# A windowed-attention and highway-FFN kernel: PSUM by a fixed plan of eight banks, and a searched order of issue

## The chip, the cores and the metric

One NeuronCore of one Trainium2 chip. The metric is the device time of one execution in microseconds (us); lower is better. The granted clock is the share of full speed that the profile gives for PE, 1.00 at full speed. The engines are PE (matmul; PEld is its weight loads), DVE (vector), ACT (scalar), POOL (GpSimd, which also issues the loads here) and SP (which issues the stores).

## The reference

```python
def _attn_ref(q, k, v):                      # q, k, v: 8 batches, 8 heads, 576 rows, 64 columns
    scores = scale * np.matmul(q, k.transpose(0, 1, 3, 2))
    ...                                      # + slope[h] * -|i - j|; only 0 <= i - j < 128 is kept
    attn = np.exp(scores - max) / sum
    return np.matmul(attn, v)

def _moe_ref(x, w_h, w_t, b_t):              # x: 4608 x 512, the attention output
    H = np.maximum(x @ w_h, 0.0)
    T = 1.0 / (1.0 + np.exp(-(x @ w_t + b_t)))
    return T * H + (1.0 - T) * x
```

## The kernel before

It works on four pairs of batches (m = 0 to 3). For each pair, Q, K and V come in by casting loads from POOL's queue; PE transposes Q and K; scores go through exp on ACT and a mask on DVE; PV gives x (after a normalising step on DVE); then each 128-row tile of x goes through the FFN: transpose (`xp`), two products (`h` with the first weight, `z` with the second, plus a bias matmul), tanh, and the elementwise rest. Each such step is a piece ("node"); a small planner inside the kernel simulates the engines and writes down one order of all pieces, and that order is what each engine executes, strictly in sequence.

PSUM is a rotating pool of four tiles of two banks each. Everything takes such a tile, also what fills one bank:

```python
psp = ctx.enter_context(tc.tile_pool(name="ps", bufs=BUFS["ps"], space=PSUM))     # BUFS["ps"] is 4

def ps_tile(dt=F32):
    return psp.tile([P, 2, 512 if dt == F32 else 1024], dt, name="ps")
...
def f_h(m, kind, gi, i):                     # a whole two-bank tile for one 128 x 512 product
    if i == 0:
        AH[m, kind, gi] = ps_tile()
    for c in range(NCK):
        nc.tensor.matmul(out=AH[m, kind, gi][:, i, :], lhsT=XT[m, kind, gi][:, i, c, :],
                         rhs=wH[:, c, :], start=c == 0, stop=c == NCK - 1)
```

The V loads, and what clears V's buffers (a column of ones, and zeros under the last, half-filled chunk):

```python
def load_v(m, c):
    n = min(P, S - c * P)
    nc.gpsimd.dma_start(
        out=VA[m % 2][0:n, c, :, :, 0:D].rearrange("s r h d -> s (r h) d"),
        in_=v[2 * m : 2 * m + 2, :, c * P : c * P + n, :].rearrange("r h s d -> s (r h) d"),
    )
def c_ones(i):
    nc.vector.memset(VA[i][:, :, :, :, D : D + 1], 1.0)
def c_vpad(i):
    nc.vector.memset(VA[i][D:P, 4, :, :, :], 0.0)
```

The softmax here doesn't subtract the row's maximum and nothing guards it: scores larger than these inputs give would overflow.

## Time and profile before

| | before |
|---|---|
| time, median of the first 3 runs | 185.03 us (184.45 to 185.9) |
| profiled span | 183.9 us |
| PE busy / idle | 155.0 / 28.9 us |
| PE idle before 41 us | 15.0 us |
| last PE matmul ends | 177.0 us |
| changes of PE's tile shape (counted in its stream) | 151 |

How to read it: the share of busy time alone says "PE, 84%". What decides is where the idle 28.9 us lie and what ended each gap; PE executes in a fixed order, so one late operand holds everything behind it. The prediction shows the lines.

### The profile page before, as it was taken

The page shows a single profiled execution, that of the slowest core. Times are in us where ns is not written, and L with a number is a line of the kernel's source. Part 1 is how long each engine was busy: PE and PEld are TensorE (multiplying, and loading weights), DVE is VectorE, ACT ScalarE, POOL GpSimd, SP SyncE. Part 2 cuts the span into 40 slices and gives each one's busy share as a digit, 9 for nine tenths or more (in the row PEclk, how much of TensorE's full clock was granted, in tenths as well). Part 3 has the DMA queues.
Part 4 walks back from the last instruction along what each step waited for, and adds up shares of the span by engine and source line. Part 5 has one row for each costly group of instructions (what it writes and reads, how often), then busy time and mean ns, then how long its engine had stood idle before and what let it go on. Part 6 is the DMA issues. An engine that isn't in the chain of part 4 may idle for free.

```text
span 183.9 us, 5244 instructions
## 1 busy us (share of the span) xinstructions
PE 155.0 (84%) x2132; PEld 93.9 (51%) x2132; DVE 141.6 (77%) x253; ACT 127.8 (69%) x178; POOL 121.5 (66%) x132
## 2 busy tenths in 40 slices
PE   0286886779999957997999999999998999999950
PEld 0264655655564524675554565665444666555510
DVE  5339885699999893697688999799899788866770
ACT  2558595753889953879779889786998888445510
POOL 7994123979999945984269953544487787667540
PEclk9999999999999996999999999999999999999995
DMA  4999999999999999999997994142212322243543
GB/s 157 225 187 198 200 199 176 138 132 92 127 207 228 210 200 205 135 187 225 208 135 96 178 159 90 45 103 61 57 45 74 93 66 74 74 103 99 137 128 94
DMA packets 70167, 25.50 MB, mean 139 GB/s; under 512 B 48128, under 2 KB 65024, under 8 KB 70144
## 3 DMA queue, kind: packets, MB, share of 16 engines
q0 software_dynamic: 62832, 14.68, 113.6%
q1 hardware_dynamic: 7312, 10.49, 21.3%
q8 instruction: 16, 0.26, 0.6%
q14 instruction: 7, 0.06, 0.1%
HBM read 30.41 MB, written 9.44 MB: 217 GB/s over the span
## 4 chain that ended last, share of the span: by engine, by line
PE 38%; DMA 26%; DVE 16%; POOL 7%; ACT 5%; issue 3%; SPq 1%; POOLq 0%; DVEq 0%; ACTq 0%
DMA kl<-in_k_dram 24%; PE ps L460 10%; PE ps L443 9%; DVE pt L363 6%; PE ps L386 6%; PE ps L270 5%; PE ps L328 5%; DVE x L403 4%; POOL ot L484 3%; DMA out_dram<-ot 3%; ACT pt L344 2%; PE ps L462 2%; DVE uu L450 2%; POOL ql L110 2%; PE ps L426 2%
## 5 line engine op out<-in xcount | busy, mean ns | idle before, releaser
L344 ACT ACTIVATE pt<-ps,bias 128x1024 bf16<-128x1024 f32 (+1 forms) x80 | 73.4, 951 | 9.1 <-PE ps L328 8.4
L484 POOL TENSOR_TENSOR ot<-uu,x 128x512 f32<-128x512 bf16 x35 | 49.7, 1421 | 30.4 <-DVE uu L478 28.9
L363 DVE TENSOR_TENSOR pt<-pt,mk 128x2048 bf16<-128x2048 bf16 (+1 forms) x40 | 47.8, 1210 | 0.7 <-ACT pt L344 0.5
L460 PE MATMUL ps<-wT,xt 128*128 128x512 bf16 x144 | 38.0, 387 | 1.2 <-DVE uu L450 0.7
L443 PE MATMUL ps<-wH,xt 128*128 128x512 bf16 x144 | 37.2, 380 | 0.6 <-DVE uu L450 0.3
L122 POOL DMA_DIRECT2D va<-in_v_dram x20 | 22.2, 1117 | 14.3 <-DMA kl<-in_k_dram 8.2
L450 DVE SCALAR_TENSOR_TENSOR uu<-ps,x 128x512 bf16<-128x512 f32 x36 | 24.8, 688 | 7.7 <-PE ps L443 7.3
L468 ACT ACTIVATE tt<-ps 128x512 f16<-128x512 f32 x36 | 21.5, 598 | 11.6 <-PE ps L462 11.1
L328 PE MATMUL ps<-qt,kt 64*128 64x256 bf16 (+2 forms) x384 | 27.2, 254 | 1.8 <-DVE kt L295 1.4
L473 POOL TENSOR_SCALAR tt<-tt 128x512 f16<-128x512 f16 x32 | 23.1, 722 | 5.6 <-ACT tt L468 5.5
L435 ACT COPY xt<-ps 128x512 bf16<-128x512 bf16 x36 | 21.0, 586 | 8.1 <-PE ps L426 7.2
L403 DVE TENSOR_TENSOR x<-ps,rd 128x256 bf16<-128x256 f32 (+3 forms) x40 | 25.5, 637 | 1.4
L386 PEld LDWEIGHTS <-pt 128*128 128x128 bf16 (+1 forms) x576 | 21.2, 101 | 8.0 <-issue 1.8
L386 PE MATMUL ps<-va,pt 128*128 128x65 bf16 (+1 forms) x576 | 24.1, 196 | 1.3 <-ACT kt L295 0.4
L295 ACT COPY kt<-ps 128x1024 bf16<-128x1024 bf16 x13 | 13.1, 1012 | 14.4 <-PE ps L270 8.4
L289 DVE COPY qt<-ps 128x1024 bf16<-128x1024 bf16 x16 | 10.9, 687 | 14.2 <-PE ps L270 10.9
L478 DVE TENSOR_TENSOR uu<-uu,tt 128x512 bf16<-128x512 bf16 x36 | 16.6, 462 | 4.9 <-POOL tt L473 2.9
L270 PE MATMUL ps<-ident,ql 128*64 128x128 bf16 (+1 forms) x320 | 13.3, 242 | 8.3 <-DMA ql<-in_q_dram 7.5
L443 PEld LDWEIGHTS <-xt 128*128 128x128 bf16 x144 | 12.1, 97 | 14.4 <-issue 2.8
L460 PEld LDWEIGHTS <-xt 128*128 128x128 bf16 x144 | 12.4, 99 | 13.7 <-issue 3.9
L328 PEld LDWEIGHTS <-kt 64*128 64x128 bf16 x384 | 12.8, 97 | 12.6 <-issue 7.0
L270 PE MATMUL ps<-ident,kl 128*64 128x128 bf16 (+1 forms) x320 | 12.8, 242 | 6.6 <-DMA kl<-in_k_dram 5.6
(46 smaller groups left out, 127.9 us busy)
## 6 DMA issues: line engine op xcount, KB each, us to landing
out_dram<-ot SPq DMA_DIRECT2D x128, 64.0 KB, 1.8
va<-in_v_dram POOLq DMA_DIRECT2D x16, 256.0 KB, 10.8
ql<-in_q_dram POOLq DMA_DIRECT2D x3, 1024.0 KB, 14.6
kl<-in_k_dram POOLq DMA_DIRECT2D x3, 1024.0 KB, 18.8
ql<-in_moe_w_h_dram SPq DMA_DIRECT2D x1, 1024.0 KB, 5.8
out_dram<-ot SPq DMA_DIRECT2D x8, 128.0 KB, 2.4
ql<-in_q_dram POOLq DMA_DIRECT2D x4, 128.0 KB, 5.8
kl<-in_k_dram POOLq DMA_DIRECT2D x4, 128.0 KB, 5.9
```

The source lines that it names most:

```text
L122: nc.gpsimd.dma_start(out=VA[m % 2][0:n, c, :, :, 0:D].rearrange("s r h d -> s (r h) d"), in_=v[2 * m : 2 * m + 2, :, c * P : c * P + n, : ...
L270: nc.tensor.transpose(out=pt[r * D : (r + 1) * D, c : c + n], in_=L[ps, r, nh * hs + hl, t * D : (t + 1) * D], identity=ident[ps, ps],)
L328: nc.tensor.matmul(out=sc[:, r, o + off : o + off + w_], lhsT=KT[i][rows, h, j * P : (j + 1) * P], rhs=rhs, start=not add, stop=not add or ...
L344: nc.scalar.activation(out=PT[m, home, h // 2][:, h % 2, :, c0 : c0 + W], in_=SC[m, kind, h][:, :, o : o + W], func=ACTF.Exp, bias=BIAS[:, ...
L363: nc.vector.tensor_tensor(out=o, in0=o, in1=mk.to_broadcast([P, 2, rep, W]), op=ALU.mult,)
L386: nc.tensor.matmul(out=av[rows, hl, n * (D + 1) : (n + 1) * (D + 1)], lhsT=pt[:, hl, r, off : off + (D if narrow else P)], rhs=va[:, j, r, ...
L403: nc.vector.tensor_tensor(out=x.rearrange("p b (h d) -> p h b d", h=2), in0=av[:, :, :, 0:D], in1=rd[:, :, 0:nb].to_broadcast([P, 2, nb, D ...
L443: nc.tensor.matmul(out=AH[m, kind, gi][:, i, :], lhsT=XT[m, kind, gi][:, i, c, :], rhs=wH[:, c, :], start=c == 0, stop=c == NCK - 1)
L450: nc.vector.scalar_tensor_tensor(out=uu[:, 0:n, :], in0=AH[m, kind, gi][:, 0:n, :], scalar=0.0, in1=x, op0=ALU.max, op1=ALU.subtract,)
L460: nc.tensor.matmul(out=az, lhsT=XT[m, kind, gi][:, i, c, :], rhs=wT[:, c, :], start=c == 0, stop=False)
L473: eng.tensor_scalar(out=tt, in0=tt, scalar1=0.5, scalar2=0.5, op0=ALU.mult, op1=ALU.add)
L484: eng.tensor_tensor(out=ot[:, 0:n, :], in0=UU.pop((m, kind, gi))[:, 0:n, :], in1=x, op=ALU.add)
```

## The change

Its intent: every PSUM bank is assigned by hand, one bank for what needs one and two neighbours for what needs two, so that more can be in flight; the planner inside the kernel goes, and a fixed order of all 762 pieces, found by a search outside, takes its place. V's buffers are to be cleared ahead of V's loads. An additive mask that nothing used is no longer built. The core of the diff:

```diff
-        "ps": 4, "pA": 5, "pB": 4, "x": 3, "xt": 5, "uu": 3, "tt": 3, "ot": 3,
+        "pA": 5, "pB": 4, "x": 3, "xt": 5, "uu": 3, "tt": 3, "ot": 3,
...
-    psp = ctx.enter_context(tc.tile_pool(name="ps", bufs=BUFS["ps"], space=PSUM))
-    def ps_tile(dt=F32):
-        return psp.tile([P, 2, 512 if dt == F32 else 1024], dt, name="ps")
+    psp = ctx.enter_context(tc.tile_pool(name="ps", bufs=1, space=PSUM))
+    PSB = psp.tile([P, 8, 512], F32, name="ps")
+    def ps_tile(nb, dt=F32):
+        b = int(next(taken))
+        v = PSB[:, b, :] if nb == 1 else PSB[:, b : b + 2, :]
+        return v if dt == F32 else v.bitcast(BF16)
...
-        if i == 0:
-            AH[m, kind, gi] = ps_tile()
+        AH[m, kind, gi] = ps_tile(1)
...
-                            lambda m=m, c=c: load_v(m, c), last_pv.get(m - 2, [])))
+                            lambda m=m, c=c: load_v(m, c),
+                            last_pv.get(m - 2, []) + [("ones", m % 2), ("vpad", m % 2)]))
...
-    order, end = plan(SHIFT, LOOKS)
+    ISSUE = """ 12 0 19 11 3 16 8 7 2 15 17 6 18 1 ... """    # 762 numbers of pieces
+    BANKS = """ 0 1 0 0 2 4 5 0 1 4 3 6 2 1 4 7 ... """        # 252 banks
+    order = [names[int(n)] for n in ISSUE.split()]
+    taken = iter(BANKS.split())
```

## The prediction

> **What bounds the kernel now.** I read the summary page first (busy shares, slices), then busy time by stretch, then the chain that ended last, then two engines' own timelines. The times are 185.03 us (184.45 to 185.9); the profiled span is 183.9, so I add 1.1 us when I go from span to time.
>
> ```profile
> PE 155.0 (84%) x2132; PEld 93.9 (51%) x2132; DVE 141.6 (77%) x253; ACT 127.8 (69%) x178; POOL 121.5 (66%) x132
> ...
> PE   0286886779999957997999999999998999999950
> ```
>
> PE is the fullest engine, but its share is a mean over stages: the row of tenths has a slow quarter at the left, a hole at slices 13 and 14, and is full to the right. The next view, busy time by stretch (per engine: busy us, instructions; last columns are granted clock, DMA share, GB/s), puts numbers on it.
>
> ```profile
> 0.00:41.00 41.00, 25.96 (x513) 19.23 (x514) 27.28 (x70) 25.60 (x43) 25.08 (x40) 1.00 1.81 180
> 41.00:60.00 19.00, 18.32 (x238) 10.32 (x236) 17.87 (x36) 14.11 (x21) 18.24 (x19) 1.00 3.26 163
> 60.00:70.20 10.20, 6.76 (x85) 3.52 (x85) 8.65 (x11) 6.60 (x9) 6.44 (x7) 1.00 1.66 206
> 70.20:90.00 19.80, 18.61 (x303) 12.33 (x304) 13.79 (x22) 14.93 (x18) 13.84 (x15) 0.91 2.12 188
> 90.00:160.00 70.00, 68.36 (x882) 39.85 (x882) 61.22 (x93) 58.26 (x75) 46.25 (x41) 1.00 0.63 94
> 160.00:177.00 17.00, 17.00 (x117) 8.65 (x115) 10.79 (x21) 8.29 (x14) 10.81 (x13) 1.00 0.45 113
> ```
>
> PE idles 15.0 us before 41 us (41.00 - 25.96), 0.7 in the next row, 3.4 in 60 to 70.2, 1.2 to 90, 1.6 from 90 to 160, none to 177, and 7 us at the end. So the front and one hole are what a better order can fill; from 90 us on there is nothing to fill, only PE time itself to shorten. The chain of waits names what the front hangs on (start, us, what):
>
> ```profile
> 10.27 18.79 DMA kl<-in_k_dram
> 29.10 1.92 PE ps L270 x32
> ...
> 51.27 18.85 DMA kl<-in_k_dram
> 70.16 0.89 PE ps L270 x16
> ```
>
> Both times it is a megabyte of K for a LATER pair of batches. The first is K of pair 1 (m=1): PE, strictly in order, stands at that transpose until 29.10, and not one PV matmul (L386) or FFN matmul (L443, L460) of pair 0 has run by then. POOL's timeline tells why no PV could have run earlier:
>
> ```profile
> 9.12 1.19 POOL L110 DMA_DIRECT2D ql<-in_q_dram  x1
> 10.27 1.18 POOL L110 DMA_DIRECT2D kl<-in_k_dram  x1
> ...
> 24.30 1.16 POOL L122 DMA_DIRECT2D va<-in_v_dram  x1 [4.81 <-DVE pt L363]
> 29.34 1.15 POOL L122 DMA_DIRECT2D va<-in_v_dram  x1 [3.88 <-DMA kl<-in_k_dram]
> ```
>
> V of pair 0 is issued behind Q and K of pair 1, at 24.30 and 29.34. The bracket names a DVE mask as releaser of the first, but the V load has no use for a mask: its waits in the program are one DMA semaphore, that of Q of pair 1 (the queue hands out eight in turn, and each DMA waits for the one eight before it), and an early DVE memset, which was done at 4 us. Q of pair 1 was issued at 9.12 and takes 14.6 us to land, which is 23.7 to 24.3. So the V loads wait for slots held by loads nobody needs yet.
>
> **What the Trainium skill says.** "DMA: Bandwidth & Descriptors", section "Anatomy of one DMA — SWDGE (gpsimd) path": DMA engines don't wait on semaphores; the issuing sequencer does, before dispatch. The trace agrees: POOL itself stands 4.81 and 3.88 us at the two V loads. "TensorEngine Tiling (Array Packing)", "Key Properties": changing the tiling mode drains TensorE. The trace agrees and gives the size:
>
> ```profile
> 142.00 0.39 PE L426 MATMUL ps<-ident,x 128*128 128x128 bf16 x4
> 142.22 1.03 PE L460 MATMUL ps<-wT,xt 128*128 128x512 bf16 x4
> ...
> 144.96 0.39 PE L426 MATMUL ps<-ident,x 128*128 128x128 bf16 x4
> 145.28 0.40 PE L328 MATMUL ps<-qt,kt 64*128 64x256 bf16 x8
> 145.61 1.04 PE L460 MATMUL ps<-wT,xt 128*128 128x512 bf16 x4
> ```
>
> Four L426 transposes take 0.22 us start to start when another 128x128 group follows and 0.32 when a 64-row group (scores) follows: 0.10 to go in. Scores of one head take 0.33; its eight matmuls are two concurrent streams of 512 columns, and four 512-column matmuls of L443 take 0.86 us start to start, so 512 columns are 0.215: 0.11 to come out. About 0.105 us a change. "PSUM — Partial Sum Buffer", "Specifications": eight banks of 2 KiB, 512 fp32. So the old tile of [128, 2, 512] fp32 takes two banks for everything, also for an FFN product or a transpose that fills one; four things fit where the new plan fits up to eight. "TensorE: Matmul & The Clock Gate", Part 1: the array runs at half clock until some 3.4 us of sustained activity. The trace agrees in durations, not in its clock column: a group of four score matmuls takes 0.54 us start to start at 19.56 and 0.32 at 92.14, though the clock reads 1.00 in both.
>
> **The change part by part.** The matmuls are the same 2132 in the same shapes; DVE loses nine instructions (the unused additive mask: 0.71 + 0.99 = 1.70 us near 15 us, beside other work).
>
> *Loads.* New order on POOL: pair 0's Q and K, then V chunks 0 and 1, the K tail, the FFN weights, then Q of pair 1, the Q tail, V chunk 2, and only then K of pair 1. In PE's stream the wait for K of pair 1 now comes after 9 PV groups (72 matmuls), 4 L426, 4 h and 3 z groups; before it came after none of them. Worth, by start-to-start times: 72 x 0.038 (12 in 0.46) = 2.7; 4 x 0.22 = 0.9; 4 x 0.86 = 3.4; 3 x 1.08 = 3.2; also 32 more score matmuls (8 x 0.33 = 2.6) and 32 more transposes (about 1.2). Together 14 us. Against it K of pair 1 lands later: three V chunks (0.79 MB), two tails (0.26) and the weights (0.52) go ahead of it, 1.57 MB at the 0.2 MB/us that the queue moves then, 7.9 us: 37 instead of 29. Net 14 - 8 = 6 us. That is credible against the room: 15.0 - 7.2 (nothing had landed before 7.2) = 7.8 us idle, plus the cold matmuls of the first 31 us (some 36 score matmuls at 0.21 per four, 1.9 us, and six groups of transposes at about 1.0 instead of 0.5, 3 us), part of which a busier PE recovers. It needs V0 by about 20 us: 3.6 MB with the fp32 weights on the other queue at 0.2 is 18 us, plus some 2 for the end. It fits.
>
> *The hole.* Q of pair 2 is now issued right behind pair 1's tails, not after five elementwise pieces of POOL, and fewer bytes are in front of K. I take 2.5 of the 3.1 us that PE waits there (70.16).
>
> *Changes of mode.* I counted the tile shape along PE's two streams: 151 changes before, 130 after. 21 x 0.105 = 2.2 us. This is the only part that shortens the full stretch from 90 on.
>
> *PSUM.* In 41 to 160 the waits of PE other than for DMA are ten waits of 0.2 to 0.8 us, 3.6 us in all, several on evacuations. Singles in place of pairs should spare some; I take 0.8.
>
> *V cleared first.* The memsets (0.12 and 0.93 us a buffer) already ran before 5.6 us and ahead of every V load; this only makes the early V loads safe. Nothing.
>
> *The end.* The last PE group is now z, not h. After h the old kernel ran u 0.69, g 0.42, out 0.69; after z come tanh 0.60, t 0.28, g, out: about +0.3.
>
> Sum: 6 + 2.5 + 2.2 + 0.8 - 0.3 = 11.2, to 173.8. A fixed order made on a model never meets all its moments, and each miss stalls an in-order engine; I give 1.5 us back: 175.3, say 175.
>
> **Rivals.** (1) *DVE or ACT becomes the bound.* For: DVE is at 61.22 of 70 us (87%) from 90 to 160, 17.87 of 19 before 60, and a mask next to POOL work stretches from 1.2 to about 2 us. Against: over the window it could use, 10 to 168 us, its 140 us are 88%, and ACT has less. If it bites, PE gets short waits for DVE all through the middle: 178 to 180. (2) *The transfers set the front anyway.* All bytes that pairs 0 and 1 need are 8.6 MB and at 0.2 that is 43 us whatever the order. For: DMA is solid until slice 23. Against: pair 0 has enough PE work to fill that time. If PE then waits for K of pair 1 or pair 2 again, only 4 of the 8.5 us come: 179. (3) *The eight banks bring coupling*: one tile in place of four could be tracked as one, serialising all. Against: PE's instructions with a wait fall from 340 to 290, and the waits name one engine each. Were it so, 200 and more; 2%. (4) *A better start*: with PE warm from 12 us, more of the cold 5 us come back: 171.
>
> **Range and chances.** 175, range 171 to 180: the low end is rival 4 with no give-back, the high end rivals 1 and 2. 2% faster is below 181.3, which needs only 3.7 of 11 us; the front alone should give it. Faster 0.91, within 2% 0.07, slower 0.02.
>
> **What would show it.** Right: first PV near 20 to 22 us (36.4 before) and first h before 26; K of pair 1 landing near 37 with PE waiting under 1 us for it; PE idle before 41 us from 15 to about 9 or 10; no wait over 1 us for K of pair 2; PE busy sum 155 to 150 to 153; last matmul at 166 to 168 in place of 177. Wrong: PE waits over 2 us for V or K at the front (loads step), over 5 us in total on DVE and ACT between 40 and 160 (rival 1), a PE busy sum unchanged (mode changes), or an end after the last matmul over 8 us.

## The result, and the profile after

175.15 us (174.14 to 175.4, 4 runs) against 184.89 us (184.45 to 185.9, 4 runs): ratio 0.9455, interval 0.9402 to 0.9509. A ratio here is the mean time of one kernel's fast runs over that of the other's fast runs of the same rounds, so it is not quite the ratio of the medians. Executions over 1.5% slower than the fastest of the same kernel are left out of the means.

The changed kernel has other line numbers: L271 is the old L270 (transposes of Q and K), L329 the old L328 (scores), L393 the old L386 (PV), L433 the old L426 (xp), L449 the old L443 (h), L465 the old L460 (z). First its page, then its busy time by stretch (engine columns as in the prediction):

```profile
PE 150.3 (87%) x2132; PEld 92.8 (54%) x2132; DVE 140.0 (81%) x244; ACT 125.4 (72%) x178; POOL 118.1 (68%) x132
...
PE   0169789999799789999999979999999999999930
```

```profile
0.00:41.00 41.00, 29.61 (x509) 19.54 (x511) 28.87 (x69) 25.65 (x46) 28.35 (x44) 1.00 1.73 180
41.00:60.00 19.00, 17.12 (x287) 10.95 (x282) 17.05 (x31) 16.82 (x23) 13.07 (x15) 1.00 2.04 186
60.00:70.00 10.00, 9.20 (x152) 6.04 (x150) 8.13 (x15) 8.43 (x11) 9.61 (x10) 1.00 3.43 138
90.00:150.00 60.00, 58.24 (x771) 35.65 (x769) 54.33 (x81) 50.90 (x68) 44.12 (x41) 1.00 0.96 105
```

PE's last matmul ends at 166.2 in place of 177.0: 10.8 us. They split into PE's idle and busy time: 3.6 us less idle before 41 us (15.0 to 11.4), 2.5 us less idle after it (7.0 to 4.5), and 4.7 us less busy (155.0 to 150.3). The end behind the last matmul is 0.4 us longer (6.9 to 7.3).

Part of the lower busy time is no matter of the order of pieces alone. The page's row of granted clock (in tenths, 40 slices), before and after:

```profile
PEclk9999999999999996999999999999999999999995
```

```profile
PEclk9999999999999999999999999999999999999995
```

The 6 is a stretch from 70.5 to 73.5 us, right behind the hole, in which the old kernel's clock reads 0.50. The five groups of matmuls from 70.16 to 74.11 take 3.95 us there, where groups of the same shapes take about 2.3 us elsewhere in that trace. So some 1.6 of the 4.7 us (an estimate from these times) are this stretch, which the changed kernel's trace does not have. Not every run of the old kernel has it to the same degree: on the chip of the yardstick run below, its fast runs at a mean granted clock of 0.987 to 0.995 took 183.1 to 183.8 us, and those at 0.979 to 0.981 took 184.5 to 185.6. What brings such stretches no run here shows.

POOL's timeline shows V issued first now (start, us):

```profile
10.12 1.18 POOL L125 DMA_DIRECT2D va<-in_v_dram  x1
...
15.35 1.16 POOL L113 DMA_DIRECT2D ql<-in_q_dram  x1 [0.21 <-issue]
...
23.81 1.16 POOL L113 DMA_DIRECT2D kl<-in_k_dram  x1 [0.96 <-DMA va<-in_v_dram]
```

and PE's timeline what it does with it: first PV at 21.36, first h at 27.45, K of pair 1 taken at 40.38 with no wait (a wait would stand in a bracket at the end of the line):

```profile
21.36 0.40 PE L393 MATMUL ps<-va,pt 128*128 128x65 bf16 x4
...
27.45 2.63 PE L449 MATMUL ps<-wH,xt 128*128 128x512 bf16 x8
...
40.38 1.08 PE L271 MATMUL ps<-ident,kl 128*64 128x128 bf16 x32
```

The hole at 70 us is gone. PE's longest waits from 41 to 160 us, before and then after (us in total, times, longest):

```profile
PE ps L270 <- DMA kl<-in_k_dram: 3.1, 1, 3.1
PE ps L256 <- ACT kt L295: 0.8, 1, 0.8
```

```profile
PE ps L329 <- DVE qt L290: 1.1, 1, 1.1
PE ps L257 <- DMA ktl<-in_k_dram: 0.9, 1, 0.9
```

Another part is the same work at a faster array. The Q and K transposes of pairs 1 to 3, before and after (the number before the comma is busy us, the one after it the mean ns):

```profile
L270 PE MATMUL ps<-ident,kl 128*64 128x128 bf16 x192 | 8.6, 244 | 4.8 <-DMA kl<-in_k_dram 4.6 <-DVE qt L289 0.2
```

```profile
L271 PE MATMUL ps<-ident,kl 128*64 128x128 bf16 x192 | 7.6, 221 | 0.0
```

With Q's (8.9 to 7.6) that is 2.3 us: the old kernel ran six of those groups before 33 us, at 0.85 to 1.07 us for sixteen matmuls, and one at the low clock behind the hole (0.89); the new one runs all of them later, at about 0.6.

### The profile page after: what moved, and what is told of

The parts are those of the page before. It is cut to its first block, busy times and chain, and to the rows that moved or that the text cites. A ratio compares the mean times of both kernels' runs of the same rounds, so it can differ in the third digit from the quotient of the medians.

```text
span 173.5 us, 5255 instructions
## 1 busy us (share of the span) xinstructions
PE 150.3 (87%) x2132; PEld 92.8 (54%) x2132; DVE 140.0 (81%) x244; ACT 125.4 (72%) x178; POOL 118.1 (68%) x132
## 2 busy tenths in 40 slices
DMA packets 70167, 25.50 MB, mean 147 GB/s; under 512 B 48128, under 2 KB 65024, under 8 KB 70144
## 4 chain that ended last, share of the span: by engine, by line
PE 53%; DMA 29%; DVE 5%; POOL 4%; ACT 3%; issue 2%; SPq 0%; POOLq 0%; ACTq 0%; DVEq 0%
DMA va<-in_v_dram 17%; PE ps L465 14%; PE ps L449 14%; DMA ktl<-in_k_dram 8%; PE ps L393 7%; PE ps L329 7%; PE ps L271 4%; PE ps L433 4%; DMA kl<-in_k_dram 3%; PE ps L467 3%; ACT pt L345 2%; DVE pt L364 1%; POOL kl L113 1%; DVE uu L456 1%; DMA out_dram<-ot 1%
## 5 line engine op out<-in xcount | busy, mean ns | idle before, releaser
L345 ACT ACTIVATE pt<-ps,bias 128x1024 bf16<-128x1024 f32 (+1 forms) x80 | 72.2, 950 | 13.5 <-PE ps L329 13.2
L489 POOL TENSOR_TENSOR ot<-uu,x 128x512 f32<-128x512 bf16 x35 | 47.7, 1365 | 24.9 <-DVE uu L483 24.8
L364 DVE TENSOR_TENSOR pt<-pt,mk 128x2048 bf16<-128x2048 bf16 (+1 forms) x40 | 46.5, 1174 | 0.8 <-ACT pt L345 0.8
L465 PE MATMUL ps<-wT,xt 128*128 128x512 bf16 x144 | 37.0, 379 | 1.0 <-DVE uu L456 0.8
L449 PE MATMUL ps<-wH,xt 128*128 128x512 bf16 x144 | 37.0, 386 | 0.3 <-DVE qt L290 0.3
L329 PE MATMUL ps<-qt,kt 64*128 64x256 bf16 (+2 forms) x384 | 24.8, 248 | 3.4 <-DVE qt L290 1.1
L478 POOL TENSOR_SCALAR tt<-tt 128x512 f16<-128x512 f16 x32 | 21.8, 687 | 7.7 <-ACT tt L473 7.5
L393 PE MATMUL ps<-va,pt 128*128 128x65 bf16 (+1 forms) x576 | 24.9, 197 | 0.8 <-DMA va<-in_v_dram 0.7
L393 PEld LDWEIGHTS <-pt 128*128 128x128 bf16 (+1 forms) x576 | 21.1, 101 | 8.2 <-issue 2.9
L483 DVE TENSOR_TENSOR uu<-uu,tt 128x512 bf16<-128x512 bf16 x36 | 19.1, 538 | 4.3 <-POOL tt L478 4.1
L449 PEld LDWEIGHTS <-xt 128*128 128x128 bf16 x144 | 13.0, 99 | 14.3 <-issue 2.1
L465 PEld LDWEIGHTS <-xt 128*128 128x128 bf16 x144 | 12.9, 98 | 13.6 <-issue 1.5
L329 PEld LDWEIGHTS <-kt 64*128 64x128 bf16 x384 | 13.2, 96 | 12.9 <-issue 8.9
L271 PE MATMUL ps<-ident,kl 128*64 128x128 bf16 (+1 forms) x320 | 12.3, 228 | 8.1 <-DMA kl<-in_k_dram 7.9
L271 PEld LDWEIGHTS <-kl 128*64 128x64 bf16 (+1 forms) x320 | 9.9, 126 | 10.1 <-DMA kl<-in_k_dram 8.4
```

The lines of the kernel that those rows point to most:

```text
L271: nc.tensor.transpose(out=pt[r * D : (r + 1) * D, c : c + n], in_=L[ps, r, nh * hs + hl, t * D : (t + 1) * D], identity=ident[ps, ps],)
L329: nc.tensor.matmul(out=sc[:, r, o + off : o + off + w_], lhsT=KT[i][rows, h, j * P : (j + 1) * P], rhs=rhs, start=not add, stop=not add or ...
L345: nc.scalar.activation(out=PT[m, home, h // 2][:, h % 2, :, c0 : c0 + W], in_=SC[m, kind, h][:, :, o : o + W], func=ACTF.Exp, bias=BIAS[:, ...
L364: nc.vector.tensor_tensor(out=o, in0=o, in1=mk.to_broadcast([P, 2, rep, W]), op=ALU.mult,)
L393: nc.tensor.matmul(out=av[rows, hl, n * (D + 1) : (n + 1) * (D + 1)], lhsT=pt[:, hl, r, off : off + (D if narrow else P)], rhs=va[:, j, r, ...
L449: nc.tensor.matmul(out=AH[m, kind, gi], lhsT=XT[m, kind, gi][:, i, c, :], rhs=wH[:, c, :], start=c == 0, stop=c == NCK - 1)
```

## The experiments

All ran beside the kernel before on the same chip. That kernel scatters more there (fast runs 181.9 to 185.6 us over three chips, slow ones up to 188.1) than the changed one (174.1 to 176.1), so I compare medians of the variants' fast runs with 175.3, which the changed kernel gave again, and use the traces for anything under 2 us. The second warm run, the rest alone, V cleared early and the six banks ran on other chips than this yardstick, so a difference under 1 us says nothing there. Where an edit is a list of numbers, the diff tells it in words.

**The changed kernel again**, the yardstick.

> The changed kernel once more, as the yardstick for the three runs beside it on the same chip: 174 to 176.

175.28 us (174.68 to 176.14, 6 runs), ratio 0.9522. The profiled run ends its last matmul at 165.7.

**Banks alone.** The order of before, PSUM as singles and pairs of eight banks.

```diff
-    ISSUE = """ 12 0 19 11 ... """          # the searched order
-    BANKS = """ 0 1 0 0 2 4 ... """
+    ISSUE = """ ... """                     # the order that the old planner gave, without the unused mask
+    BANKS = """ ... """                     # at each piece the bank or pair that has been free longest
```

> The order of issue of the kernel before (without its nine unused mask instructions), but PSUM handed out as single banks and pairs from eight, least recently freed first. My theory (PSUM itself is worth under 1 us, DVE's nine instructions nothing much): 183.5 to 185, PE busy about 155, PE still standing at K of pair 1 until about 29 us. Rival (the eight banks are what lets PE run ahead, so they are the gain): 179 or less, PE's waits for evacuations between 41 and 160 us down from 3.6 us to under 1.

183.67 us (183.66 to 185.0), ratio 0.9983, interval 0.9882 to 1.0084: no gain that could be told from nothing. PE busy is 155.9. The old order never holds more than six banks' worth at once, so it has no use for more than six.

But the clock was not the same. In this run's trace it reads mostly 0.50 from 29 to 43.5 us and again from 73.5 to 77.5:

```profile
PEclk9999997558999999699999999999999999999995
```

PE's work from the transposes of K of pair 1 to the first h takes 15.3 us there (28.39 to 43.64) in place of 12.2 (29.10 to 41.34), and K of pair 2 is taken 2.3 us later (72.42 against 70.16). From there to the last matmul, the same pieces in the same order take 104.0 us in place of 106.9, with 0.9 us of PE idle in place of 2.8. So the banks may well spare the old order some waits (in part perhaps because that stretch begins later); the total does not show it, and what they are worth at an equal clock stays open. The other three runs, too, had a mean granted clock (0.960 to 0.976) below that of the kernel before (0.979 to 0.995 in its fast runs).

**The new order with less PSUM.** Two runs: four pairs as in the old pool, then six banks with singles allowed. In both, a piece that finds no free bank is put off until the one that frees it has been issued.

```diff
+    # four pairs: each thing takes a pair (the Q and K transposes of a part share one), 14 places of PE's order move
+    # six banks: singles and pairs as in the changed kernel, out of banks 0 to 5, 21 places of PE's order move
```

> The changed kernel's order with the old PSUM: four pairs of banks, one thing in each (Q and K transposes of a part share a pair, as before). 14 places of PE's order had to give way, since the changed order holds up to twelve pairs' worth at once. The first experiment showed that banks alone give nothing to the old order. My theory as predicted (0.8 us for PSUM): 175.5 to 177. Rival (the banks give nothing to the old order, but the new order cannot be had without them): 179 or more, with waits of PE for evacuations (ACT exp, DVE) above 5 us in all between 41 and 160 us.

> The changed order with singles and pairs as now, but out of six banks in place of eight; 21 places of PE's order give way, and which bank goes to what is chosen by the longest free. The four-pairs run, 276 us, could be the loss of the new order's capacity or the waste of a pair for every single. Theory (the waste: most things need one bank, so six singles still carry most of the order): 177 to 190. Rival (the order needs the whole capacity, any shortage chains PE to DVE and ACT): over 200.

272.1 us (three fast runs, 271.71 to 274.39; three slow ones up to 280.5) and 220.1 us. For the first my theory falls and the rival stands; for the second too: six singles do not carry most of the order. The changed order holds all eight banks at its peak; with a pair for each thing it would hold six pairs, twelve banks (the "twelve pairs' worth" expected above should have been this). With fewer, PE waits for evacuations all through; the longest of the six-bank run (us in total, times, longest):

```profile
PE ps L329 <- ACT pt L345: 11.1, 12, 1.4
...
PE ps L393 <- ACT pt L345: 4.2, 5, 1.2
PE ps L329 <- DVE x L410: 3.9, 8, 1.1
```

Not all of the loss is waiting: PE's busy time is 181.9 us and 160.8 us in place of 150.3, and some 26 and 7 us of these are lost to a lower clock (an estimate: busy time by half microseconds, times the share of full speed that the clock column lacks). But PE's idle time is 88.5 and 57.2 us in place of 23.2, which is most of it. So banks and order are not two terms of a sum: the banks gave the old order no gain that its time shows, and the new order, squeezed into fewer, is far slower than the old one. What these runs do not tell is how good an order made for four pairs, with V loaded early, could be; the orders here were only squeezed, not planned again.

**Front alone.** The changed order up to PE's first use of K of pair 1 (158 pieces), then the order of before.

```diff
-    ISSUE = changed order
+    ISSUE = changed order up to the transposes of K of pair 1, then the remaining pieces in the order of before
```

> The changed kernel's order up to the point where PE first needs K of pair 1, with its banks; from there the order of the kernel before, banks least recently freed. My theory (front worth 6, hole 2.5 of which the loads of pair 2 stay as before, mode changes 2.2 mostly later): 178 to 180. Rival A (all the gain is the front): 175 to 176. Rival B (the front gives little, the rest is one better order): 182 or more.

180.46 us (three fast runs, 179.74 to 181.27; a fourth, 182.78, is slow), ratio 0.9793. A little above what I expected: the front gives about 4 us of the 10, and the rest of the order gives the other 5 to 6. Its trace says what differs from the changed kernel: from 41 to 70 us PE idles 4.8 us (29.0 - 16.57 - 7.62) against 2.7, and PE's busy time is 154.9 with 155 changes of tile shape. But the clock reads 0.50 from 44.5 to 48.5 and from 62 to 65.5 us, which by the column costs some 3.2 us of that busy time; the other runs' mean clock was as low (0.971 to 0.976). So the split of 4 and 5 to 6 is rough, and the front may be worth more.

**Rest alone**, the reverse.

```diff
-    ISSUE = changed order
+    ISSUE = order of before up to the transposes of K of pair 1, then the remaining pieces in the changed order
```

> The reverse of the front-only run: the order of the kernel before, loads and all, up to where PE first needs K of pair 1; from there the changed order, banks least recently freed. If front and rest add up (front 2.8 us by the front-only run against the banks-only run, rest 5.6): 177.5 to 179. Rival (the rest of the new order only pays when the early FFN work of the front is done): 181 or more. My prediction's own split (front 6) would give 180 to 181.

186.76 us, ratio 1.0189: slower than either kernel. The parts do not add up. Its trace has a wait of 8.9 us for V: the changed order goes to PV at once, while the old front's loads bring V late. So the run repeats the stall of the next one, and does not measure the rest.

**V behind pair 1 again.** Two of POOL's loads moved, nothing else.

```diff
-    V chunks 0 and 1, ... , Q of pair 1, ... , V chunk 2, K of pair 1
+    Q of pair 1, K of pair 1, V chunks 0 and 1, ... , V chunk 2
```

> The changed kernel with only Q and K of pair 1 issued ahead of V of pair 0 again, all else in its place. My theory (V lands near 35 in place of 21, and PE, in order, stands at the first PV): a wait of PE for V of some 12 to 14 us at 21, of which part is won back because K of pair 1 is there early: 182 to 188. Rival (transfers are solid until 41 us anyway, so their order does not matter): 175 to 177.

183.3 us (182.92 to 183.45): 8 of the 9.7 us are given back by the place of two loads. PE's timeline has the wait where it was expected:

```profile
31.31 0.38 PE L393 MATMUL ps<-va,pt 128*128 128x65 bf16 x4 [10.77 <-DMA va<-in_v_dram]
```

**Changes of tile shape.** The bias matmul, whose rows 1 and up are zero, on 64 rows.

```diff
-        nc.tensor.matmul(out=az, lhsT=ones1[:], rhs=bT[:], start=False, stop=True)
+        nc.tensor.matmul(out=az, lhsT=ones1[0:64, :], rhs=bT[0:64, :], start=False, stop=True)
```

> The changed kernel with the bias matmul on 64 rows in place of 128 (rows 64 and up of its operands are zero, so the result is the same): no work is added, but each of the 36 z groups gets two changes of tile shape, 72 in all. My theory (0.105 us each, PE full past 41 us): 72 x 0.105 = 7.6 us, of which some 7 show: 181.5 to 183, PE busy up by about as much. Rival (a change of shape is hidden under the weight loads): 175 to 176.

177.67 us (177.5 to 178.15), ratio 0.9648. I had miscounted: where scores, of the same shape, follow a z group, no change is added but one is moved, so the stream has 181 changes in place of 130, 51 more and not 72. PE's busy time rose from 150.3 to 154.7, which is 4.4 / 51 = 0.086 us a change, and the span by 2.3 us (173.5 to 175.8), because PE idles 2.1 us less: 0.5 before 41 us, 1.1 between there and its last matmul, 0.5 behind it. The timeline of this run, then that of the changed kernel: the bias matmul to the next group takes 0.32 us start to start (148.63 to 148.95) in place of 0.21 (141.25 to 141.46).

```profile
148.63 0.39 PE L467 MATMUL ps<-bT,ones 64*128 64x512 bf16 x1
148.95 1.04 PE L465 MATMUL ps<-wT,xt 128*128 128x512 bf16 x4
```

```profile
141.25 0.38 PE L467 MATMUL ps<-bT,ones 128*128 128x512 bf16 x1
141.46 1.03 PE L465 MATMUL ps<-wT,xt 128*128 128x512 bf16 x4
```

**A warm array at the front.** Two runs with dummy matmuls (results thrown away).

```diff
+        nc.vector.memset(wz[:], 1.0)
+        warm(12)                            # second run: warm(19)
         for key in order:
             nodes[key][3]()
+            if key[0] == "tr" and n < N7:   # second run: 3, 4, 2 and 12 behind four chosen groups
+                warm(3)
```

> The changed kernel with 12 dummy 128x128 by 512 matmuls while PE waits for the first load, and 3 more behind each group of Q and K transposes at the front, into a bank not yet in use, so that the array is at full clock when the front's real work comes. In the changed kernel a group of four score matmuls still takes 0.54 us start to start until 27 us and the first eight h matmuls 2.46 us in place of 1.73. Theory A (the front is cold array time): 2 us or more faster, 173 or less. Theory B (the front is set by the loads: K of pair 1 landed at about 39 to 40, when PE came for it at 40.4): PE does its front work earlier, then stands 1 to 3 us at K of pair 1; gain under 1.5 us: 173.7 to 175.5.

> As the warm run, but with dummy matmuls only where PE waits anyway: 19 before the first load has landed, then 3, 4, 2 and 12 in the gaps between the first groups, so that the front's real work is neither late nor cold. In the warm run PE crossed the stretch from its first score behind V to K of pair 1 in 17.6 us in place of 19.6, but started it 2.3 us late. Theory A (front is cold array time): 172.5 to 173.5. Theory B (K of pair 1 and the other loads set the front's end at about 39 to 40 us): PE is there by about 38 and stands 1 us or more for a load, gain 0 to 1.3 us: 173.8 to 175.3.

175.56 and 176.31 us: no gain in either. The dummies do warm the array: the first 32 transposes take 0.69 us in place of 1.06. But it did not stay warm. In the first run the clock column falls to 0.50 from 9 to 16 us, and three dummies take 1.39 us start to start in place of 0.75; PE starts PV at 23.40 in place of 21.36 and comes to K of pair 1 at 40.68, much as before. In the second it falls from 17.5 to 21 and from 27.5 to 31.5 us: twelve dummies meant for 3 us took 4.08, the first eight h matmuls 2.42, no better than the 2.46 of the changed kernel, and PE comes to K at 42.88, 2.5 us late. The first run's clock row, then the second's:

```profile
PEclk9956999999999999999999999999999999999995
```

```profile
PEclk9999696999999999999999999999999999999996
```

So these runs do not test theory A: no front was warm throughout. My second set of numbers, gain 0 to 1.3 with a wait at K, was not met either, and neither run was early at K. What the second one shows is that the front has some slack: 2.5 us late at K are 0.8 at the last matmul (167.0 against 166.2).

**An earlier start.** The first FFN weight (1 MB of fp32 on SP's queue at 0.81 us, cast on ACT) on POOL's queue behind V chunk 1, cast by the transfer.

```diff
-        nc.sync.dma_start(out=w_stage()..., in_=moe_w_h...)     # first of all, then a cast on ACT
+        load_w(0)                                               # on POOL's queue behind V chunk 1
```

> The changed kernel with the first FFN weight loaded on the same queue as the rest, cast by the transfer, behind V chunk 1, in place of a 1 MB fp32 load on SP's queue at 0.81 us that runs beside the first Q and K loads (and ACT's cast of 1.9 us falls away). The same bytes move before K of pair 1. Theory A (PE starts late because the first loads share the engines with it): first transposes at about 5 in place of 6.8 and 8.1 us, 1 to 2.5 us faster: 172.5 to 174. Theory B (the front as a whole is set by all its bytes up to K of pair 1): an early start is lost again at K: 174.5 to 176.

177.68 us (176.92 to 178.52), 2.4 slower than the yardstick, worse than both theories. PE did start early, at 4.61 in place of 6.77, and yet reached its first PV at 21.01 against 21.36: the loads of the second half of Q and K set that moment. From there it fell behind: PE waited 2.2 us for V where the changed kernel waits 0.7, with the weight now ahead of the later loads on the casting queue. In the first 41 us the transfers ran at 161 GB/s in place of 180, 0.78 MB less; but 0.52 MB of that is only that the weight counts as bf16 and no longer as fp32. So theory B is right that an early start is lost again, and the fp32 load on the other queue was the better way for this weight by the time; why is not shown.

**V cleared early**, both buffers at the start of DVE's order.

```diff
-    DVE: ..., clear V buffer 0, ... (front) ..., clear V buffer 1 in two places
+    DVE: clear V buffers 0 and 1, ... (front) ...
```

> The changed kernel with both V buffers cleared at the start of DVE's order, as before, in place of the second one's memsets (0.12 and 0.93 us) in the middle of the front. My prediction (nothing): 174.7 to 175.7. Rival (the place of the clearing matters to DVE at the front): off by 1 us or more.

175.13 us (three fast runs, 174.72 to 175.65; the profiled run, 177.47, is slow, so its trace is not compared): nothing, as expected.

No version here beats the changed kernel.

## Why the prediction was right or wrong

The total, 175, was met (175.15), and most of its causes too, but in part by luck: the loads' 6 us came about in another way than the sum says, the banks' part was misread, and 1.6 us came from a low clock behind the hole that no term had. (The 1.1 us from span to time mixed two runs; the profiled one took 185.63, which is 1.7 above its span.)

*Loads, 6 us: right in cause, met in size by luck.* Idle before 41 us fell by 3.6, and some 2.0 us of the lower busy time are transposes of the front that now run at full speed, 5.6 together. The sum itself, 14 us of work less 8 of delay, was off on both sides. PE's stream has 64 PV matmuls ahead of the transpose of K of pair 1 (not 72), 28 more scores, which take 1.05 us (not 32 in 2.6), and 16 more transposes (not 32); priced as in the prediction, all of it is about 11.6 us. And that transpose begins 11.3 us later (40.38 against 29.10), not 8. There the changed kernel is hardly ahead. The gain lies behind it: between 29.10 and 41.30 the old kernel still idled 2.0 us and lost some 1.7 to slow transposes and scores, which the prediction had named only as room. Undoing the order of two loads gives back 8 us, more than this term, because PE's new order then stands at V for 10.8 us; the front alone gives about 4. Two of its moments were off: the first h came at 27.45, not before 26, in a stretch where matmuls were still slow (the first eight h took 2.46 us start to start, and 1.73 later), and PE came for K of pair 1 at 40.4, where I had it landing at 37. That load took 15.2 us to land; issued at 23.81, that is 39. The two delays hid each other, so the wait at K stayed away.

*The hole, 2.5 us, and PSUM's 0.8: together 2.5.* The 3.1 us wait for K of pair 2 went completely, but new small ones came (1.1, 0.9, 0.8), so idle after 41 us fell by 2.5 in place of 3.3. The low clock behind that wait (some 1.6 us) went with it; the prediction's own table shows it as 0.91 for 70.2 to 90 us, and no term took it up.

*Changes of shape, 2.2 us: nearly.* 21 x 0.086 = 1.8 of PE's busy time. On the end it must be less: 51 more changes moved the span by 2.3 us only. That each of the 21 counted in full was the mis-sized part.

*PSUM, 0.8 us: the step that was wrong in kind.* I treated the banks as a small separate saving of waits. As such they gave no gain in time that could be measured, though the banks-only trace has some 2 us less PE idle past the hole. What I missed is that this order cannot run as it stands without them: 220 us with six banks, 272 with four pairs. I had the means to see it: counting what is live along the changed order (eight banks at its peak, six pairs where four exist) needs no chip.

*The end, +0.3: +0.4. V cleared first, nothing: nothing.*

*Rivals.* DVE did come nearer to its limit (54.33 of 60 us, 91%, from 90 to 150) but PE's waits for DVE and ACT from 41 to 160 us are 2.8 us in all, so rival 1 did not bite. Rival 2, transfers, is half true of the front: the chain that ended last now lies on loads until 57.7 us (start, us, what):

```profile
11.81 11.31 DMA va<-in_v_dram
...
26.31 17.49 DMA va<-in_v_dram
44.09 13.60 DMA ktl<-in_k_dram
```

That fits the early-start run, where PE's gain at the front did not come through to the end. The better start of rival 4 was tried and gave nothing, but the warm runs did not stay warm, so a warm front stays untested. What stays open: how the 4.7 us of busy time split. The low clock behind the hole (1.6), the transposes of the front (2.0) and the shapes (1.8, scaled from another run) are 5.4, more than 4.7; against them stand slow matmuls that the changed kernel has at its own front (the first eight h alone are 0.7 over). No run isolates any of them.

## What to carry to other kernels

When an engine runs in a fixed order, look at which load each of its waits needs and whether something that could run now stands behind it: two loads in the wrong place cost 8 us here, and the bracket in the trace named the wrong releaser. Count what is live in PSUM along an order before calling buffers a side matter; more banks brought no gain in time to the order that was not made for them, and the order that was, squeezed into fewer, fell far behind. Where the front is set by transfers, an earlier start there was lost again at the next loads. And read the granted clock beside every difference of busy time: here it fell to 0.50 for 3 us and more in some kernels' traces and not in others, and it left open what the banks-only run and both warm runs were made to show.

## What the Trainium skill lacked or had wrong

- "TensorEngine Tiling (Array Packing)", "Key Properties", says that a change of tiling mode drains TensorE but gives no cost: here 0.10 to 0.11 us start to start, and 0.086 us of PE busy time each over 51 added changes.
- "TensorE: Matmul & The Clock Gate", Part 4, says that the full clock does not engage for transposes. Here the same transposes run at two speeds: 1.06 and 0.69 us for 32 of 64x64 (the changed kernel and the first warm run), 1.06 and 0.64 us for 16 of 128x128 (both in the kernel before). Whether transposes help to warm the array up no run here shows.
- The same page, Part 1, gives some 3.4 us of sustained work for warming up, and does not say how much work with short gaps counts as sustained. In the changed kernel the array stayed slow much longer: groups of four score matmuls took 0.54 us start to start until 27 us, with PE at work from 6.8 us on and no wait over 1.2 us behind the first transpose, while the trace's clock column read 1.00.
- "DMA: Bandwidth & Descriptors", "Anatomy of one DMA — SWDGE (gpsimd) path", fits a load from POOL with 2.0 us plus bytes over 436 GB/s; the loads here, nearly all casting and one behind another, moved 180 GB/s over the first 41 us of the changed kernel, counted, for the casting loads, in the bf16 bytes written (the fp32 read for them is twice that). No page says what a cast in the transfer costs, and no run here tells it from the cost of small packets (48128 of the 70167 are under 512 B).
- No page says how much slower an order of issue becomes when it is run with fewer PSUM banks than it was made for: 272 us on four pairs and 220 us on six banks against 175 us on eight, in part at a lower clock.
